# A fused chunk-selected attention and SwiGLU kernel: hand-woven instruction order replaced by a list-scheduled order with explicit buffers, with 64x64-tile chunk bounds and 256-token FFN blocks

## The chip, the cores and the metric

The kernel runs on one core of one Trainium2 chip. The metric is the device time of one execution in microseconds (us), and lower is better. Every execution has a state: fast, or slow when it is over 1.5% longer than the fastest execution of the same kernel; a single execution has none. A kernel is called faster or slower only where the whole 95% interval of its ratio lies more than 2% from 1. "Span" is the time from the first to the last instruction of the profiled execution; it is about 1.7 us shorter than the device time.

The engines are named as in the profile: PE is TensorE (matmuls) and PEld its weight loads, DVE is VectorE, ACT is ScalarE, POOL is GpSimd, SP is SyncE, which issues most of the loads and all of the stores. The program gives each engine its instructions in a fixed order; the second dip below shows GpSimd standing still for 4.96 us with a later instruction ready.

## The reference, cut to what matters

There are 4 batches, 8 heads, 768 tokens and 64 elements per head. Keys are in 24 chunks of 32. Each query attends to at most 6 chunks, those with the largest upper bound of the score. The result, as 3072 tokens of 512, goes through RMS normalisation and a SwiGLU layer of width 1536.

```python
k_min, k_max = min and max of k over each chunk of 32 tokens
ub = np.sum(np.maximum(q * k_min, q * k_max), axis=-1)      # one bound per query and chunk
ub = np.where(causal, ub, -1e9)
top_chunks = np.argsort(ub, axis=-1)[..., -6:]
scores = q @ k.T / 8, masked to the chosen chunks and to the past
attn = softmax(scores);  x = attn @ v
xn = x / sqrt(mean(x * x) + 1e-6) * rms_g
out = (silu(xn @ w_gate) * (xn @ w_val)) @ w_out
```

The unit of work is a *job*: 256 tokens of one batch and 4 of its heads (24 jobs). Two jobs make one 256-token *block* (12 blocks), and a block that has been through attention can go through the FFN.

## The kernel before

Loads come as 2 KB runs per partition (8 tokens of 64 elements), VectorE transposes them to head dimension by token, and GpSimd or ScalarE makes a bf16 copy.

```python
in_=src[b, 4 * g + a, BLK * m:BLK * (m + 1), :].rearrange(
    "(r j) d -> r (j d)", r=32, j=8)                       # 2 KB runs
...
def p_transpose(j, nm):
    nc.vector.transpose(
        out=st[j][nm + "T"].rearrange("p h (r j) -> p j h r", r=32, j=8),
        in_=st[j][nm + "raw"][:])
```

The chunk bounds are a product of queries with a block-diagonal matrix BD of the chunks' minima and ranges, in fp32, on the whole 128x128 array. Four heads use 32 rows each, so three quarters of BD are zeros.

```python
def p_upper(j):
    for t in range(4):
        rhs = st[j]["qT"][:, t, BLK - w:] if t < 2 else st[j]["qR"][:, t - 2, :]
        nc.tensor.matmul(ubp[:, 0:w], bd[:, t, :], rhs, start=(t == 0), stop=(t == 3))
```

The FFN works on 256 or 512 tokens at a time. Its matmuls are cut into *slices* (one gated pair of columns, or one projection), and the main loop puts one slice after each piece of attention work, by hand:

```python
CHUNKS = [(0, 1), (1, 1)] + [(2 + 2 * i, 2) for i in range(4)] + [(10, 1), (11, 1)]   # blocks
...
for i in range(2, NU):                 # units of attention, batch after batch
    need(nxt); scores(nxt)
    sl = next_slice(i)
    sl and sl.part()                   # FFN matmuls on PE
    if nxt: exps(nxt, 0)
    prep()                             # transposes, bounds and ranking of a later job
    sl and sl.part()
    if nxt: exps(nxt, 1)
    sl and sl.rest()
    run_later()                        # normalisation of a finished block, some steps later
    ...
    values(u, 0, avn, [kg], pts)
    if last: normalise(u, 0, avn)
    ...
```

The softmax here doesn't subtract the row's maximum and nothing guards it: scores larger than these inputs give would overflow.

## Time and profile before

The kernel took 366.86 us, the median of three executions (366.36 to 367.74; 366.89 with a fourth that was run beside the changed kernel).

| Engine | busy, us | share of span |
|---|---|---|
| PE | 308.3 | 84% |
| DVE | 216.1 | 59% |
| POOL | 201.1 | 55% |
| ACT | 198.7 | 54% |

These are the lines of its page that the argument rests on. The first is busy time, share and instruction count per engine. The next three cut the span into 40 slices of 9.1 us and give, in tenths, the busy share of PE, the clock granted to PE, and the share of the DMA engines.

```profile
PE 308.3 (84%) x3132; PEld 197.0 (54%) x3168; DVE 216.1 (59%) x539; ACT 198.7 (54%) x321; POOL 201.1 (55%) x327
PE   0255597889969799799879997999999999999995
PEclk9999978996998999999969999999999999999999
DMA  7999955536243233222430321210000200011001
```

PE is the bound, but it does little in the first five slices, where the DMA engines are full, and it has gaps until about slice 25. A busy PE is also not a PE at its rate. The timeline of PE shows the same eight matmuls early and late (start, length, group, and in brackets the idle time before and what ended it):

```profile
32.66 1.87 PE L397 MATMUL gp<-xsT,wg 128*128 128x256 bf16 x8 [1.31 <-DVE xsT L376]
...
93.05 1.05 PE L397 MATMUL gp<-xsT,wg 128*128 128x256 bf16 x8
```

The late group is followed by the next one 0.89 us after its start, so eight such matmuls cost 0.87 to 0.89 us when the array is warm, and about twice that at 32 us. The Trainium skill ("TensorE: Matmul & The Clock Gate", Part 1) says that the array starts at half its clock and gets the full one after some 3.4 us of sustained work. The trace agrees in the ratio; no run here isolates the 3.4 us.

I therefore use a second measure beside busy time, called *work*: each matmul counted at its warm, back-to-back duration from this trace (0.109 us for 256 columns on the full array, 0.216 for 512, and so on; for the new bounds, which it does not have, the figure in the change). The program has 272 us of such work. In a stretch of time, work over length is the *efficiency*, and length minus work is the *loss*, which contains idle time and half-rate time alike. Before, the loss is 365.2 - 272 = 93 us. (The 272 counts the eight narrow bounds jobs, of 64 columns, in proportion to their columns, at 0.43 us; the trace shows 0.84 us for a warm one, at 139.60 us. The work is thus nearer 275 us and the loss nearer 90. The prediction and the sums below keep 272 and 93; where the 3 us matter, it is said.)

The last line needed here is a group of VectorE (line, operation, shapes, count, then busy us and mean ns):

```profile
L179 DVE STREAM_TRANSPOSE kT<-kraw 128x512 f32<-128x512 f32 x24 | 26.3, 1096 | 0.4 <-DMA kraw<-in_k_dram 0.4
```

### The profile page before, as it was taken

How to read it: one execution, taken by the hardware profiler on the slowest of the kernel's cores; microseconds unless marked ns; L12 is line 12 of the kernel's file. 1: busy time of each engine (PE TensorE's matmuls, PEld its weight loads, DVE VectorE, ACT ScalarE, POOL GpSimd, SP SyncE). 2: the span in 40 equal slices, each digit the busy share in tenths (PEclk: the TensorE clock that was granted, in tenths of full speed). 3: DMA queues.
4: the chain of work that ended last, by engine and by line, in shares of the span. 5: the costliest groups of instructions: out<-in, count | busy, mean ns of one | idle time of the engine just before them, and what ended most of it. 6: DMA issues, size and time to landing. Idle time of an engine off the chain costs nothing.

```text
span 365.2 us, 8414 instructions
## 1 busy us (share of the span) xinstructions
PE 308.3 (84%) x3132; PEld 197.0 (54%) x3168; DVE 216.1 (59%) x539; ACT 198.7 (54%) x321; POOL 201.1 (55%) x327
## 2 busy tenths in 40 slices
PE   0255597889969799799879997999999999999995
PEld 0243375556856465455554554556546555548682
DVE  6336726677786787775576887538875144404130
ACT  2322444455744557684429576456783588735461
POOL 6362454636785556866347768339874064713361
PEclk9999978996998999999969999999999999999999
DMA  7999955536243233222430321210000200011001
GB/s 155 193 205 196 208 146 148 133 87 177 62 111 84 75 108 89 65 58 74 154 102 22 83 59 29 86 61 2 2 2 30 86 3 2 2 72 44 31 31 57
DMA packets 43305, 30.44 MB, mean 83 GB/s; under 512 B 29440, under 2 KB 34048, under 8 KB 43264
## 3 DMA queue, kind: packets, MB, share of 16 engines
q1 hardware_dynamic: 38160, 24.66, 24.6%
q0 software_dynamic: 4720, 4.72, 8.1%
q8 instruction: 25, 0.41, 0.5%
q10 hardware_dynamic: 384, 0.52, 0.4%
q14 instruction: 16, 0.13, 0.1%
HBM read 28.31 MB, written 6.29 MB: 95 GB/s over the span
## 4 chain that ended last, share of the span: by engine, by line
PE 63%; DVE 10%; DMA 10%; ACT 9%; issue 3%; POOL 2%; SPq 1%; DVEq 0%; ACTq 0%; POOLq 0%
PE op L420 16%; PE gp L397 14%; PE vp L397 13%; PE ubp L231 8%; DMA vraw<-in_v_dram 6%; PE sc L278 5%; PE avn L317 4%; DMA kraw<-in_k_dram 3%; ACT junk L346 3%; ACT th L404 3%; ACT pt L297 2%; DVE tg L410 2%; PE sc L283 2%; DVE qT L179 1%; PE tp L374 1%
## 5 line engine op out<-in xcount | busy, mean ns | idle before, releaser
L297 ACT ACTIVATE pt<-sc 128x768 bf16<-128x768 f32 (+1 forms) x96 | 85.7, 913 | 77.4 <-PE sc L283 77.2
L414 POOL TENSOR_TENSOR hh<-tg,vs 128x512 bf16<-128x512 bf16 x72 | 83.4, 1158 | 60.9 <-ACT vs L407 52.8
L410 DVE SCALAR_TENSOR_TENSOR tg<-th,gp 128x512 bf16<-128x512 bf16 x72 | 49.3, 685 | 69.2 <-ACT th L404 63.1
L397 PE MATMUL vp<-xsT,wv 128*128 128x512 bf16 (+1 forms) x384 | 77.2, 336 | 3.8 <-DVE tg L410 3.4
L397 PE MATMUL gp<-xsT,wg 128*128 128x256 bf16 (+1 forms) x361 | 76.4, 341 | 2.2 <-DVE xsT L376 1.3
L420 PE MATMUL op<-wo,hh 128*128 128x512 bf16 x275 | 64.2, 379 | 1.1 <-issue 0.3
L397 PEld LDWEIGHTS <-wv 128*128 128x128 bf16 x384 | 39.0, 102 | 30.9 <-issue 5.1
L407 ACT ACTIVATE vs<-vp 128x512 bf16<-128x512 f32 x72 | 43.2, 600 | 13.5 <-PE vp L397 12.1
L404 ACT ACTIVATE th<-gp 128x512 bf16<-128x512 f32 x72 | 43.1, 599 | 10.9 <-PE gp L397 10.4
L397 PEld LDWEIGHTS <-wg 128*128 128x128 bf16 x384 | 35.3, 103 | 22.6 <-issue 5.6
L301 POOL TENSOR_SCALAR_AFFINE_SELECT pt<-pt 128x512 bf16<-128x512 bf16 x48 | 31.1, 651 | 28.6 <-ACT pt L297 22.3
L420 PEld LDWEIGHTS <-hh 128*128 128x128 bf16 x288 | 26.7, 98 | 31.5 <-POOL hh L414 1.3
L317 PEld LDWEIGHTS <-pt 128*128 128x128 bf16 x672 | 31.2, 101 | 19.7 <-DVE xnat L332 5.2
L278 PE MATMUL sc<-qb,kb 32*128 32x256 bf16 (+1 forms) x768 | 35.8, 272 | 2.3 <-ACT pt L297 2.3
L427 ACT ACTIVATE osb<-op 128x512 f32<-128x512 f32 x24 | 14.3, 597 | 41.4 <-PE op L420 35.2
L283 PE MATMUL sc<-mt,chunkrow 32*128 32x256 bf16 (+2 forms) x384 | 25.1, 259 | 7.5 <-DVE mt L256 7.5
L179 DVE STREAM_TRANSPOSE kT<-kraw 128x512 f32<-128x512 f32 x24 | 26.3, 1096 | 0.4 <-DMA kraw<-in_k_dram 0.4
L179 DVE STREAM_TRANSPOSE qT<-qraw 128x512 f32<-128x512 f32 x24 | 26.4, 1098 | 0.0
L331 DVE RECIPROCAL rden<-avn 128x4 f32<-128x4 f32 x48 | 8.4, 175 | 29.5 <-PE avn L317 29.3
L278 PEld LDWEIGHTS <-kb 32*128 32x128 bf16 x768 | 16.3, 96 | 12.0 <-issue 9.2
L218 POOL TENSOR_SCALAR qraw<-qT 128x512 f32<-128x512 f32 (+1 forms) x24 | 12.3, 512 | 18.5 <-DVE qT L179 13.4
L231 PE MATMUL ubp<-qT,BD_180 128*128 128x256 f32 (+1 forms) x48 | 12.3, 385 | 10.9 <-POOL BD_180 L206 6.8
(129 smaller groups left out, 368.8 us busy)
## 6 DMA issues: line engine op xcount, KB each, us to landing
vraw<-in_v_dram SPq DMA_DIRECT2D x48, 128.0 KB, 2.7
out_dram<-osb SPq DMA_DIRECT2D x24, 256.0 KB, 2.1
kraw<-in_k_dram SPq DMA_DIRECT2D x92, 64.0 KB, 2.3
qraw<-in_q_dram SPq DMA_DIRECT2D x92, 64.0 KB, 1.9
wg<-in_moe_w_gate_dram POOLq DMA_DIRECT2D x3, 512.0 KB, 6.8
wv<-in_moe_w_val_dram POOLq DMA_DIRECT2D x3, 512.0 KB, 9.4
wo<-in_moe_w_out_dram POOLq DMA_DIRECT2D x1, 1536.0 KB, 22.3
kraw<-in_k_dram ACTq DMA_DIRECT2D x4, 64.0 KB, 2.3
```

Of the source, the lines that this page charges most:

```text
L179: nc.vector.transpose(out=st[j][nm + "T"].rearrange("p h (r j) -> p j h r", r=32, j=8), in_=st[j][nm + "raw"][:],)
L231: nc.tensor.matmul(ubp[:, 0:w], bd[:, t, :], rhs, start=(t == 0), stop=(t == 3))
L278: nc.tensor.matmul(o, st[jk]["kb"][r, t, ks], st[jq]["qb"][r, t, q0:], start=(t == 0), stop=False, skip_group_check=True,)
L283: nc.tensor.matmul(o[:, m0 - q0:], chunkrow[r, BLK * kg + P * e:BLK * kg + P * (e + 1)], st[jq]["mt"][r, m0:], start=False, stop=True, ski ...
L297: nc.scalar.activation(out=pt[:, hs, 0:W], in_=u["sc"][hp][:, :, 0:W], func=ACT.Exp, scale=SCALE)
L317: nc.tensor.matmul(avn[:, a, :], pts[kg][:, a, off:off + P], vext[:, e, a, :], start=(kb == 0 and a == 0), stop=(kb == nkb - 1 and a == 3) ...
L397: nc.tensor.matmul(ps[:, i * W:(i + 1) * W], w[:, g, ht * P:(ht + 1) * P], x[:, g, 0:W], start=(g == 0), stop=(g == NP - 1), skip_group_ch ...
L404: nc.scalar.activation(out=th[:], in_=gp[:], func=ACT.Tanh, scale=0.5)
L407: nc.scalar.activation(out=vs[:], in_=vp[:], func=ACT.Copy, scale=0.5)
L410: nc.vector.scalar_tensor_tensor(out=tg[:], in0=th[:], scalar=1.0, in1=gp[:], op0=ALU.add, op1=ALU.mult,)
L414: nc.gpsimd.tensor_tensor(out=hh[hp][:], in0=tg[:], in1=vs[:], op=ALU.mult)
L420: nc.tensor.matmul(op[:], hh[ht // K][:, o:o + P], wo[:, ht, :], start=(ht == 0), stop=(ht == NHT - 1),)
```

## The change

The intent is to fill PE's idle time. The change writes down every operation with an engine, an estimated duration, its inputs and its buffers, and lets a small scheduler inside the kernel play the program through before anything is emitted. At each step it takes, on the engine that can start first, the operation of best priority among those that can start at once. It also models the DMA rings, so that the order accounts for when loads land. The order that results is fixed; on the chip, engines and semaphores follow it. With that come four other changes: blocks are taken in a free order over the batches (small ones of all four batches first), FFN blocks are always 256 tokens (the first in two halves), the bounds use 64x64 tiles, and keys and queries from the fourth block on are loaded as 256 B runs in an element order that VectorE transposes faster.

```diff
+class Plan:
+    def run(self, in_order=()):
+        ...
+        while len(order) < len(self.ops):
+            best = None
+            for e, c in cand.items():
+                rows = [(est(o, e), o) for o in c]          # earliest start of each candidate
+                t0 = max(at[e], min(t for t, o in rows))
+                t, o = min(((t, o) for t, o in rows if t <= t0 + 1e-9),
+                           key=lambda r: (r[1].pri, r[1].seq))
+                if best is None or (t0, o.pri) < (best[0], best[1].pri):
+                    best = (t0, o, e)
+            ...
+            o.start = t; at[e] = t + o.occ; o.done = t + o.lat
+            if o.dma is not None:
+                rings.add(t + o.occ + 0.8, e, packets, cost, o)   # lands 1.0 us after its last packet
...
-    order = [(b, m, g) for b in range(B) for m in range(NBLK) for g in range(NG)]
+    ORDER = [(0, 0), (1, 0), (2, 0), (3, 0), (0, 1), (1, 1), (0, 2), (2, 1), (1, 2),
+             (3, 1), (2, 2), (3, 2)]
+    PACE, LEAD = 23.0, 60.0
+    SPLIT = {0}                  # the first block goes through the FFN in halves
+    PACKED = {0, 1, 2}           # blocks loaded as 2 KB runs; the others as 256 B runs
...
+        occ = {"SP": 0.46, "ACT": 0.46, "POOL": 0.9}[eng]          # modelled issue time of a DMA
...
-                    "(r j) d -> r (j d)", r=32, j=8),
+                        "(j r) d -> r j d", r=32)                  # 256 B runs, 16 packets of 0.022
...
-            nc.tensor.matmul(ubp[:, 0:w], bd[:, t, :], rhs, start=(t == 0), stop=(t == 3))
+            for t in range(4):
+                for hp in range(2):
+                    for c in range(2):
+                        TE.matmul(o[64 * c:64 * (c + 1), hp, 0:32 * nj],
+                                  d[64 * hp:64 * (hp + 1), t, :],
+                                  qs[t // 2][64 * hp:64 * (hp + 1), t % 2, :, c, :], ...)
...
+            plan.op(f"scale{i}{s}", "DVE", 0.265, 0.35, ...)        # each operation with occupancy
+            o = plan.op(f"{nm}{U}.{hp}", "PE", 0.873, 1.035, ...)   # and latency, in us
...
+    for o in plan.run(in_order=("kraw", "qraw", "vraw", "kT", "qT", "kb", "qb", "VX", ...)):
+        o.fn()
```

With 64x64 tiles the masks come out in two operands of half the width, one of which needs a copy between partitions (`swap`), so the mask matmuls are twice as many and half as wide. Eighteen of the 72 gate products move from GpSimd to VectorE.

## The prediction

> **What bounds the kernel now.** I costed every TensorE instruction of the old program at the warm, back-to-back duration that the instruction groups and timeline show: gate/value matmuls 0.109 us (256 columns) or 0.216 (512), projection 0.216, a four-at-a-time score or mask matmul 0.027, a value matmul 0.032, a 256-column fp32 bounds job 1.73. That is 272 us of a span of 365.2: TensorE is the bound, yet for 93 us it is idle, cold or throttled. By stretches of time, the work done is 10.6 us in 0-50, 35 in 50-100, 36 in 100-150, 71 in 150-240, 53 in 240-300, 19 in 300-320: efficiencies of 0.21, 0.70, 0.72, 0.79, 0.89, 0.95. In the first 45 us the DMA engines are full (share 0.9 to 1.2), the first FFN matmul comes at 32.7 us, and matmuls run at half rate (eight take 1.82 us until 49 us, 0.87 later). VectorE, ScalarE and GpSimd are busy 54 to 59%: none binds.
>
> **What changes.**
> 1. Bounds: 64x64 tiles, four at once, 128 columns instead of 256. This line is 8% of the chain of waits (31 us in total); I estimate half, so 12 to 15 us less, nearly all critical.
> 2. Masks cover only needed columns, from two half-width operands: no more PE time, twice the instructions.
> 3. FFN in 256-token blocks (the first in halves): same columns, 1248 weight loads instead of 768, hidden at 0.87 us per eight: +1 us. PE work becomes about 258 us. Tiling-mode changes on PE rise from 95 to 139 in instruction order; at about 0.1 us each, +4.5 us.
> 4. VectorE: key/query transposes in another element order, costed by the change at 0.6 us (1.1 now): 18 us less if right. 18 products move from GpSimd (1.16 us) to VectorE; swap copies and 16 more ScalarE row operations cost some 15 us. VectorE rises to about 75% of the shorter span; none binds.
> 5. Loads from block 4 on come as 256 B runs instead of 2 KB: more DMA time, harmless later, where the share is 0.2 to 0.4.
> 6. The order: small blocks of four batches first, FFN from about 18 us, every engine list-scheduled. This is the large term. Later loads wait behind weights, so I expect 15 us of PE work by 40 us: a loss of 25 us, against 39 in the first 50 today; afterwards efficiency 0.93, which the old kernel reaches only late.
>
> **Sum.** 40 + (258-15)/0.93 = 301, plus output copy and store (0.6 + 2.1 us) and some throttling: **307 us**, 80% range **296 to 322**. Faster by over 2%: 0.96; within 2%: 0.03; slower: 0.01.
>
> The Trainium skill ("TensorE: Matmul & The Clock Gate", Part 1) says matmuls start at half clock and reach full rate after about 3.4 us of sustained work; the trace agrees (1.82 against 0.87 us per eight).
>
> **What would show it.** Bounds matmuls near 16 to 19 us; eight 256-column matmuls still 0.87 us; efficiency above 0.9 from 50 us on, PE about 90% busy in the slices after the sixth; span minus PE work about 48 us instead of 93. If step 6 is wrong, middle slices show PE idle with waits on VectorE or ScalarE.
>
> **What would make it wrong.** The order is fixed from modelled durations: if VectorE or GpSimd run longer than modelled, or weights land later, in-order queues pass the delay on (over 320). If the clock stays up and gaps vanish, 295.

## The result, and the profile after

The changed kernel took 323.72 us, the median of four executions (322.84 to 324.64), against 366.89 us for the kernel before. The ratio is 0.8824, with a 95% interval of 0.8803 to 0.8846. Ratios here are the mean time of one kernel's fast runs over that of the other's of the same rounds, so they are not quite the ratio of the medians quoted. The direction and most of the size were as predicted; the time was 16.7 us above the predicted 307 and 1.7 us above the range.

These are the same lines of the page after; a slice is now 8.1 us.

```profile
PE 290.6 (90%) x4624; PEld 218.8 (68%) x4624; DVE 219.5 (68%) x613; ACT 219.3 (68%) x393; POOL 150.8 (47%) x270
PE   0459959989999997699999999999999999999894
PEclk9999969999999999799999999999999999999999
DMA  8999977666587567740120130100100100100101
```

PE is full from slice 18 (about 140 us) on. Two dips stand out before that: the sixth slice (40 to 48 us), where the granted clock is also low, and slices 16 and 17 (near 130 us). The transposes, which the by-shape view gives, and the wait list of PE (what waited, for what, total us, times, longest) are:

```profile
L487 DVE STREAM_TRANSPOSE kT<-kraw 128x512 f32<-128x512 f32 x24 | 18.6, 794 | 5.8 <-DMA kraw<-in_k_dram 5.4 <-POOL kb L495 0.2
```

```profile
PE S L618 <- ACT qb L494: 11.4, 1, 11.4
PE F L754 <- DVE xs L744: 5.1, 4, 2.5
PE F L824 <- POOL hh L814: 5.1, 1, 5.1
```

The first wait is the start of the program. The other two hold the two dips. Here is the first of them in PE's timeline:

```profile
43.03 0.61 PE L754 MATMUL F<-ident,xs 128*128 128x128 bf16 x4 [2.47 <-DVE xs L744]
44.19 0.61 PE L754 MATMUL F<-ident,xs 128*128 128x128 bf16 x4 [0.55 <-DVE xs L744]
45.36 2.32 PE L792 MATMUL F<-xsT,wg 128*128 128x256 bf16 x8 [0.56 <-ACT xsT L763]
47.47 2.97 PE L824 MATMUL F<-wo,hh 128*128 128x512 bf16 x8
...
55.79 1.04 PE L792 MATMUL F<-xsT,wv 128*128 128x256 bf16 x8
```

PE waits for the second block's normalisation, and then runs its next groups at half rate: eight gate matmuls take 2.1 us to the start of the next group, where the warm group of the same shape takes 0.87. The profile's chain of waits (`--critical`) leads from there back to a load of keys; three of its pieces (start, length):

```profile
32.20 7.20 DMA kraw<-in_k_dram
39.42 1.27 DVE kT L487 x2
41.91 0.41 DVE xs L744
```

The load landed at 39.40 us, and VectorE transposed its keys before it scaled the block that PE waited for. But GpSimd's step of the same normalisation ended only at 41.71 us, 0.2 us before the scalings, so the load is not shown to be the only cause.

The second dip needs three engines' timelines. PE:

```profile
125.69 1.06 PE L694 MATMUL F<-VX,pt 128*128 128x65 bf16 x28
131.84 4.30 PE L824 MATMUL F<-wo,hh 128*128 128x512 bf16 x12 [5.08 <-POOL hh L814]
```

GpSimd, for which PE waits:

```profile
123.92 0.61 POOL L495 CAST kb<-kT 128x512 bf16<-128x512 f32 x1
129.50 1.17 POOL L600 CAST VX<-vraw 128x512 bf16<-128x512 f32 x2 [4.96 <-DMA vraw<-in_v_dram]
130.63 1.15 POOL L814 TENSOR_TENSOR hh<-tg,vs 128x512 bf16<-128x512 bf16 x1
```

And SyncE, which issues the load that GpSimd waits for:

```profile
112.34 6.22 SPq L365 DMA_DIRECT2D kraw<-in_k_dram  x8
118.67 5.09 SPq L365 DMA_DIRECT2D qraw<-in_q_dram  x8
123.86 1.14 SPq L365 DMA_DIRECT2D vraw<-in_v_dram  x2
```

Read from the bottom: SyncE issued the value load of block (3, 1) at 123.86 us, after sixteen key and query loads that held it for 11.3 us: thirteen of them for 0.38 to 0.46 us each, three for 1.50 to 1.72 us. GpSimd had the two value casts in front of the gate product `hh` in its queue, so it sat 4.96 us with work that could have run (the product's last input, from ScalarE, was there at 124.8 us). PE needed that `hh` for its projection, stood for 5.08 us, and then ran twelve projections in 4.30 us, where twelve warm ones take 2.6.

The scheduler's own plan is a useful second trace, since its starts can be printed when the kernel is built. It has that value load issued at 109.5 us (14.4 us earlier) and the whole program done at 307.1 us. Comparing PE's starts of projections and of block transposes with the plan, the chip is 1.5 us late at 23 us, 7 to 9 us late from 51 to 124 us, 16 us late from 138 us, and 15.6 us late at the last projection: it lost nothing more to its plan in the last 180 us. SyncE was already 10.3 us late when the sixteen loads began (112.34 us against 102.05). Part of that came through the first dip: SyncE stood still for 2.7 and 1.0 us before the stores at 77.37 and 80.77 us, whose output PE had made about 7 us late. That is read from the timeline and was not tested.

The accounting of work by stretch (computed from PE's groups in each stretch as said above; matmuls across a boundary count in both):

| Stretch, us | work | efficiency | loss |
|---|---|---|---|
| 0 to 40 | 15.8 | 0.40 | 24.2 |
| 40 to 60 | 12.5 | 0.62 | 7.5 |
| 60 to 120 | 52.8 | 0.88 | 7.2 |
| 120 to 140 | 12.8 | 0.64 | 7.2 |
| 140 to 300 | 151.1 | 0.94 | 8.9 |
| 300 to end | 16.8 | 0.73 | 6.1 |

In total the work went from 272 to 260.5 us and the loss from 93 to 62 us. So of the 42 us of span, 11 are less work and 31 are less loss; with the narrow bounds jobs at their measured 0.84 us, 15 and 28.

### The profile page after: what moved, and what is told of

It is laid out like the page before. It is cut to its first block, busy times and chain, and to the rows that moved or that the text cites. A ratio compares the mean times of both kernels' runs of the same rounds, so it can differ in the third digit from the quotient of the medians.

```text
span 322.9 us, 11287 instructions
## 1 busy us (share of the span) xinstructions
PE 290.6 (90%) x4624; PEld 218.8 (68%) x4624; DVE 219.5 (68%) x613; ACT 219.3 (68%) x393; POOL 150.8 (47%) x270
## 3 DMA queue, kind: packets, MB, share of 16 engines
q1 hardware_dynamic: 69712, 24.66, 31.3%
## 4 chain that ended last, share of the span: by engine, by line
PE 64%; DMA 11%; DVE 9%; ACT 5%; SPq 4%; issue 3%; POOL 3%; DVEq 0%; POOLq 0%; ACTq 0%
PE F L792 29%; PE F L824 16%; DMA kraw<-in_k_dram 6%; PE S L549 5%; PE S L618 5%; PE F L694 5%; DMA vraw<-in_v_dram 4%; SPq L365 4%; PE S L629 2%; PE F L754 2%; DVE kx L502 1%; DVE xs L744 1%; POOL hh L814 1%; DVE kT L487 1%; ACT pt L668 1%
## 5 line engine op out<-in xcount | busy, mean ns | idle before, releaser
L668 ACT ACTIVATE pt<-S 128x1024 bf16<-128x1024 f32 (+3 forms) x100 | 86.5, 889 | 17.9 <-PE S L629 15.5
L792 PE MATMUL F<-xsT,wg 128*128 128x256 bf16 (+1 forms) x624 | 77.5, 269 | 1.5 <-ACT xsT L763 1.1
L792 PE MATMUL F<-xsT,wv 128*128 128x256 bf16 (+1 forms) x624 | 75.6, 267 | 0.5 <-DVE xnat L713 0.3
L824 PE MATMUL F<-wo,hh 128*128 128x512 bf16 x288 | 69.9, 390 | 5.1 <-POOL hh L814 5.1
L803 DVE SCALAR_TENSOR_TENSOR tg<-th,F 128x512 bf16<-128x512 bf16 x72 | 48.7, 677 | 34.9 <-ACT th L799 34.7
L799 ACT ACTIVATE th<-F 128x512 bf16<-128x512 f32 x72 | 43.6, 606 | 11.9 <-PE F L792 10.1
L618 PE MATMUL S<-qb,kb 32*128 32x256 bf16 (+1 forms) x784 | 34.5, 259 | 12.4 <-ACT qb L494 11.4
L811 ACT ACTIVATE vs<-F 128x512 bf16<-128x512 f32 x54 | 32.9, 609 | 6.2 <-PE F L792 4.3
L502 DVE TENSOR_REDUCE kx<-kT 128x16 f32<-128x512 f32 x48 | 30.3, 663 | 0.0
L694 PE MATMUL F<-VX,pt 128*128 128x65 bf16 x672 | 27.7, 195 | 2.2 <-ACT vs L811 0.9
L487 DVE STREAM_TRANSPOSE kT<-kraw 128x512 f32<-128x512 f32 x24 | 18.6, 794 | 5.8 <-DMA kraw<-in_k_dram 5.4
```

Source lines behind the costliest of these rows:

```text
L502: plan.op(f"ext{n}{J}", "DVE", 0.585, 0.67, lambda n=n, op=op: VE.tensor_reduce(out=at(kx)[:, n], in_=at(kT).rearrange("p h (c t) -> p h c ...
L618: TE.matmul(s[a // 2][:, a % 2, c0:c0 + q1 - q0], kbt[r, t, ks], qbt[r, t, q0:q1], start=(t == 0), stop=(t == 1 and not mask), skip_group_ ...
L668: lambda pt=pt, hs=hs, c0=c0, c1=c1, x=sc[hp]: SE.activation(out=at(pt)[:, hs, c0:c1], in_=at(x)[:, :, c0:c1], func=ACT.Exp, scale=SCALE), ...
L694: TE.matmul(o[:, a, :], p_[:, a, off:off + P], vt[:, e, a, :], start=(kb_ == 0 and a == 0), stop=(kb_ == nkb - 1 and a == 3), skip_group_c ...
L792: TE.matmul(at(p_)[:, n * W:(n + 1) * W], w[:, g, ht * P:(ht + 1) * P], at(xT)[:, g, 0:W], start=(g == 0), stop=(g == NP - 1), skip_group_ ...
L799: plan.op(f"tanh{U}.{hp}", "ACT", 0.48, 0.6, lambda th=th, gp=gp: SE.activation(out=at(th), in_=at(gp), func=ACT.Tanh, scale=0.5), pri, re ...
```

## The experiments

Three questions were open. Which part of the change brought the gain? Where did the 16.7 us go that I had not expected? And were the two dips accidents, or signs of something in the plan? My first theory was that the two dips cost their length and that the value load behind GpSimd's queue made the second. The rivals were that the 256 B runs slow everything, that the array's cold clock does, and that the plan's figures for loads make it too hopeful everywhere.

All runs gave the reference's results. Runs of different sets were each timed against the kernel before on their own chip, so ratios are compared between sets. Not tested apart were the FFN blocks of 256 tokens, the eighteen moved gate products, and the explicit buffers, which all variants of the new kernel share.

### The value casts behind the urgent product

```diff
+    order = plan.run(...)
+    late = [o for o in order if o.name in ("vx(3, 1, 0)", "vx(3, 1, 1)")]
+    order = [o for o in order if o not in late]
+    at_ = [o.name for o in order].index("hh(3, (0, 1)).5") + 1
+    order[at_:at_] = late
```

> One place of GpSimd's queue is changed: the two value casts of block (3,1), which waited for a load until 129.5 us, go behind the gated product hh that TensorE waited for (126.8 to 131.8 us). Theory A (an operation that is not urgent, but stands first in an in-order queue and waits for a late load, holds up the product): the 5.1 us wait shrinks to about 2 (the product's other input was ready at 127.3), the half-rate matmuls after it go, and the time falls from 323.7 by 4 to 6, to 318 to 320. Rival B (all engines wait for the late loads anyway): at most 1.5 less.

Measured: 322.1 us as the median of all four executions; the three fast ones took 321.56 to 322.37, with a median of 321.82. The ratio is 0.877 (0.8725 to 0.8816), against 0.8824. The profiled execution was the other one, and it was slow: 726.4 us. A profile of that tells nothing about the swap, so the kernel was run again for one look.

> The kernel of e1 again, for a trace of its fast state (the first one fell into an execution of 726 us). e1 gained 1.6 us, not 4 to 6. If another operation in an in-order queue, waiting for the same late loads, took over: TensorE's wait at 127 us is shorter than 5.1 us, and VectorE (next for it: a key transpose that waited for a load until 131.2 us) or GpSimd makes it wait again within 20 us, in sum about 5 us. If the wait was as long as before, the product had another reason.

Measured: 320.88 us in one execution (so its state is unknown, but it lies beside e1's fast ones), a span of 319.1. GpSimd's queue now runs the product first, and waits less long for the values:

```profile
123.89 1.15 POOL L814 TENSOR_TENSOR hh<-tg,vs 128x512 bf16<-128x512 bf16 x1 [0.45 <-ACT vs L811]
126.29 1.17 POOL L600 CAST VX<-vraw 128x512 bf16<-128x512 f32 x2 [1.25 <-DMA vraw<-in_v_dram]
```

PE's 5.1 us wait is gone, but a new one has come a little later in its timeline:

```profile
132.58 0.77 PE L754 MATMUL F<-ident,xs 128*128 128x128 bf16 x8 [2.01 <-DVE xs L744]
```

(My first expectation was wrong on when the product could run: the input that I had seen at 127.3 us belongs to the next block.) The loss between 120 and 140 us fell only from 7.2 to 5.1 us, or to 4.7 with the two projections that this trace's records lack there. So the mechanism of the second dip is shown, and its worth is about 2 us, not the 7 that PE's trace shows there: when one wait was taken away, the next thing that was late took its place. As a cause of the miss, then, the second dip by itself accounts for about an eighth of the 16.7 us.

As for the slow execution, its page has this as busy time, and its timeline has the following group of gate matmuls:

```profile
PE 702.4 (97%) x4624; PEld 395.3 (55%) x4624; DVE 218.2 (30%) x613; ACT 228.3 (32%) x393; POOL 150.5 (21%) x270
...
400.07 2.64 PE L792 MATMUL F<-xsT,wg 128*128 128x256 bf16 x8
```

All other engines have their usual busy time, while groups of eight gate matmuls took 2.1 to 2.5 us from start to start, 2.4 to 2.8 times the warm 0.87, from 60 us to the end. The clock recorded for it is 1.00. (The record is not always silent: of the kernel before, one execution in the same set was slow as well, 476.65 us, at a recorded clock of 0.671.) Nothing is concluded from these two executions for the change.

### The schedule's figures for loads

Only numbers of the scheduler's model change: the time that SyncE needs for an issue, the time of a packet in a ring for the 256 B runs, and the time from the last packet to the landing. The work of every engine stays the same, apart from operations that the plan may give to one of two engines.

```diff
-            op.done = now + 1.0
+            op.done = now + 1.5
-        occ = {"SP": 0.46, "ACT": 0.46, "POOL": 0.9}[eng]
+        occ = {"SP": 0.60, "ACT": 0.46, "POOL": 0.9}[eng]
-                        "r j h d -> r j (h d)"), 16, 0.022))
+                        "r j h d -> r j (h d)"), 16, 0.032))
```

> Only the schedule's model of loads is changed, to what the trace shows: 0.60 us of SyncE per load instead of 0.46, a ring packet of 256 B runs 0.032 instead of 0.022, landing 0.5 us later. No instruction is added or taken away; the order changes. Its own model ends at 303.6 us (307.1 with the old figures). Theory A (the stall at 127 us comes from a load model that is too fast): no wait over 2 us on TensorE between 100 and 300 us, and 310 to 316. Rival C (the mid stall is not a matter of the load model): 320 to 325.

Measured: 313.96 us (313.18 to 314.61), ratio 0.8552 (0.8513 to 0.8592), about 10 us less than the changed kernel. PE's slices have neither dip:

```profile
PE   0469979997999999999999999999999999998994
```

No wait on PE after 100 us is over 2 us. The start of the second block's FFN comes 3.1 us earlier and at full rate (VectorE now scales that block at 38.60 us, ahead of the two key transposes):

```profile
42.26 1.03 PE L792 MATMUL F<-xsT,wg 128*128 128x256 bf16 x8 [1.67 <-DVE xsT L767]
```

By the same accounting, the loss fell from 7.5 to 3.1 us in 40 to 60 and from 7.2 to 1.2 us in 120 to 140, and stayed within 1.1 us of the old value in the other stretches up to 300 us. That is where the two dips were. The two parts of the edit were then run apart.

> Of e2's three figures only the first: 0.60 us of SyncE per load instead of 0.46. The model ends at 307.1 us. If the issue time of SyncE is what the old model missed: 312 to 317. If it is the time in the rings and to landing: 320 to 325, with a wait of TensorE of 2 us or more between 60 and 160 us.

Issue time alone: 320.24 us (318.41 to 322.0), ratio 0.8699 (0.8648 to 0.8751).

> Of e2's three figures only the other two: a ring packet of 256 B runs 0.032 instead of 0.022 us, landing 1.5 us after the last packet instead of 1.0. The model ends at 303.7 us (e2: 303.6). If the rings are what matters: 311 to 316 as e2. If the issue time is: 320 to 325.

Packet and landing time alone: 312.69 us (312.16 to 315.27), ratio 0.8524 (0.8474 to 0.8575). So these two figures, which were not run apart, do nearly all of it, and the issue time alone brings 3.5 us (4.6 by the ratios). By the accounting of work, the issue time alone takes away the second dip (1.3 us of loss from 120 to 140) but not the first (6.9 us from 40 to 60), and from 140 to 300 it loses 3.5 us more than the changed kernel: taking away the second dip is again worth less than its length. The wait of 2 us or more between 60 and 160 us that I had expected with such a time did not come; the longest is 1.5 us. Packet and landing time alone leave 4.1 and 2.6 us of loss in the two stretches.

I had thought of these figures as the truer ones, and the profile bears that out only in part. How long a load of keys holds SyncE in the changed kernel, in ns (shortest, median, longest), is in this line:

```profile
L365 SPq DMA_DIRECT2D kraw<-in_k_dram x82: 311/448/3311, 1.3 to 136.0; - x82
```

So 0.46 was right for most loads: 140 of SyncE's 164 key and query loads took 0.50 us or less. The mean is 0.55 us, and my 0.6 was such a mean of groups of eight; 18 loads of 0.8 to 3.3 us raise it. What held those, the profile does not show. And the page's mean time of a packet on the hardware queue of the changed kernel is 31.3% of 16 engines' 322.9 us over 69,712 packets, which is 23 ns, close to the old 0.022; and the median time from issue to landing of a key load is 2.6 us, which is what the old model gives too (0.46 + 0.8 + 16 x 0.022 + 1.0). What the model lacks, by these figures, is the tail: the few long issues, and loads that wait for their turn. Making every load later in the plan is a stand-in for it. Whether a truer model of the queues would do better than a uniformly pessimistic one, no run tells.

### All keys and queries in 2 KB runs

```diff
-    PACKED = {0, 1, 2}
+    PACKED = set(range(12))
```

> All blocks load keys and queries as 2 KB runs with 4 transfers per tensor, as blocks 0 to 2 do, instead of 256 B runs with 8; the transposes of blocks 3 to 11 take 1.1 us instead of 0.7 on VectorE. If the 256 B runs and the number of transfers make SyncE late (it was 14 us behind its plan at 124 us): SyncE keeps its plan, no stall at 127, about 312 to 317. If VectorE is the tighter one up to 130 us (busy 80 to 100%): 321 or more, with waits on VectorE.

Measured: 322.94 us (322.29 to 323.39), ratio 0.8797 (0.8757 to 0.8836): the same as the changed kernel within the intervals. VectorE is busy for 238.3 us instead of 219.5, because the slower transposes come back, and the stall at 127 us does not appear. Thus the 256 B runs, as such, are not the cause of the miss: without them the same time is lost in other places (7.9 us of loss from 40 to 60, and 11.5 instead of 8.9 from 140 to 300). The result lies in the range that I had given for VectorE as the tighter engine, but PE's waits for VectorE's scalings (`xs`) are 6.3 us instead of 5.1, too little to show it. The faster transpose of the 256 B runs brings nothing in the end either.

### The bounds, twice

```diff
-            for t in range(4):
+            for t in list(range(4)) * 2:
-        o = plan.op(f"upper{J}", "PE", 0.925 if m else 0.49, 1.09 if m else 0.66, ...)
+        o = plan.op(f"upper{J}", "PE", 1.85 if m else 0.98, 2.02 if m else 1.15, ...)
```

> The 64x64 bounds matmuls are issued twice (same result, the accumulation is started again), and the schedule is told so: 18.7 us more TensorE work by the plan's figures, bounds then cost about what the 128x128 form did (31 us). If TensorE bounds the kernel after 40 us: 11 to 18 us more, 335 to 342. If its work hides in gaps: under 5 more.

Measured: 336.28 us (334.05 to 337.0), ratio 0.9146 (0.9083 to 0.9208), which is 12.6 us more (11.8 by the ratios). The bounds' busy time on PE rose from 23.9 to 43.9 us, which happens to be what they had in the kernel before (43.8). By the plan's figures that is 18.7 us more work (16 jobs of 0.925 and 8 of 0.49). So about two thirds of bounds work shows in the time, in the new order, where the scheduler had been told of it.

### The old kernel with the new bounds

The old kernel's order was kept, and the 64x64 bounds, the half-width masks and the copies between partitions (on VectorE) were put into it. Its diff is long; this is the core.

```diff
-            nc.tensor.matmul(ubp[:, 0:w], bd[:, t, :], rhs, start=(t == 0), stop=(t == 3))
+            for hp in range(2):
+                for c in range(2):
+                    nc.tensor.matmul(ubp[hp][64 * c:64 * (c + 1), 0:32 * nj],
+                                     bd[64 * hp:64 * (hp + 1), t, :],
+                                     qs[t // 2][64 * hp:64 * (hp + 1), t % 2, :, c, :],
+                                     start=(t == 0), stop=(t == 3))
...
+        nc.vector.tensor_copy(mto[0:64, 0:nj], mtd[64:128, 0, 0:nj])
+        nc.vector.tensor_copy(mto[64:128, 0:nj], mtd[0:64, 1, 0:nj])
```

> The old kernel with one part of the change: bounds on 64x64 tiles (two PSUM banks, swap copies on VectorE, masks from two half-width operands); order and all else as before. TensorE loses 12 to 15 us of bounds work, VectorE gains about 12 us. If the bounds matmuls were critical in the old order (8% of its chain of waits): 8 to 13 us less, 354 to 359. If its gaps would swallow it: within 4 us of 367.

Measured: 373.7 us (371.08 to 376.1), ratio 1.0204 (1.0138 to 1.0269): longer by 1.4 to 2.7%, so not clearly more than 2%. Both of my ranges had it shorter or within 4 us. The page shows the exchange:

```profile
PE 301.9 (82%) x4091; PEld 190.0 (51%) x4128; DVE 240.1 (65%) x627; ACT 198.7 (54%) x321; POOL 198.4 (54%) x327
```

PE is busy for 6.4 us less than before, VectorE for 24 us more. By PE's wait list, waits on VectorE's `xnat` grew from 5.4 to 8.1 us, and those on `tg` before the bounds grew from one of 1.2 us to nine of 4.9 us in all. One caution is that the bounds here take two of the three PSUM banks that they share with the FFN, where the changed kernel has them elsewhere; the extra banks may be part of the loss. What is shown is that this part of the change, put into the old order in this form, brings no gain, and costs some us.

### Batches in order

```diff
-    ORDER = [(0, 0), (1, 0), (2, 0), (3, 0), (0, 1), (1, 1), (0, 2), (2, 1), (1, 2), (3, 1), (2, 2), (3, 2)]
+    ORDER = [(b, m) for b in range(B) for m in range(NBLK)]
```

> The new kernel with its blocks in the order of the old one (batch after batch), list-scheduled by the same model, whose end is 306.6 us (307.1 in free order). If the free order over batches is a large term: 333 or more, as large attention blocks come while the weights are still landing. If the list schedule makes up for the order: within 6 us of 323.7.

Measured: 323.1 us (322.0 to 323.84), ratio 0.8801 (0.8756 to 0.8846). The free order over the batches, which the change names first, is worth nothing that these runs can see. The same order was also run with the later loads of the second experiment:

> The batch order of e7 with the load model of e2; its own model ends at 306.7 us (e7: 306.6). e2 may have won 10 us because its load model is nearer to the chip, or because any new order is a new draw. If the load model: this run comes 5 to 11 us below e7's 323.1, at 312 to 318, and TensorE has no stretch of 20 us between 60 and 300 us that loses over 3.5 us. If it was a draw: within 4 us of 323.

Measured: 315.31 us (314.9 to 315.83), ratio 0.8611 (0.8576 to 0.8646), 7.8 us less than the 323.1 of its pair (7.0 by the ratios, which count here, as the two ran on different chips). By its trace the stretch from 80 to 100 us loses 5.4 us, more than the 3.5 that I had allowed; but 21 projections, 4.5 us of work, are missing from its records, so that half of the expectation stays open. A new plan changes the order everywhere, so one gain of 10 us might have been a lucky draw. This second draw, from another order of blocks, speaks against that.

### Filling PE's early gaps with idle work

Wherever the plan leaves PE idle for over 0.5 us before 60 us, matmuls of the identity with itself are put in front of the next group that takes a fresh PSUM buffer; they are overwritten.

```diff
+        if o.eng == "PE":
+            gap, end = o.start - end, o.start + o.occ
+            if gap > 0.5 and o.start < 60.0 and o.takes:
+                ...
+                for _ in range(int((gap - 0.2) * 0.8 / 0.107)):
+                    TE.matmul(x, ident[:], ident[:], start=True, stop=True, skip_group_check=True)
```

> The new kernel with idle TensorE time before 60 us filled by matmuls whose result is overwritten (identity times identity, into the PSUM slot that the next operation fills), about 80% of each gap of the plan over 0.5 us. If part of the 31 us lost in the first 50 us is half clock after idling: eight 256-column matmuls at 45 us take 1.0 to 1.3 us instead of 2.3, the first 128-column groups 1.06 instead of 1.89, and 3 to 6 us less, 318 to 321. If the start is bound by loads and chains of small operations alone: within 1.5 us of 323.7.

Measured: 321.7 us (319.72 to 323.02), ratio 0.8761 (0.8703 to 0.8819). The first FFN matmuls now run at full rate (sixteen of 128 columns in 1.05 us, where they took 1.89), but the group at 45.39 us still takes 2.32 us, since the fillers there were too few. The time is 2 us less, but the intervals overlap, and it misses the 318 to 321 that I had expected. So filling these gaps is not shown to bring anything, and what the half rate after 42 us costs was not tested.

### A plan that knows no durations

```diff
+            o.occ, o.lat = 0.6, 0.8      # for every operation, in the model only
```

> The new kernel with a schedule that is blind to durations: every operation is taken to last 0.6 us (0.8 to its result); order of blocks, priorities, loads and work are unchanged. If modelled durations are what the list schedule lives on: TensorE waits all along, 335 or more. If priorities, many small operations and explicit buffers do it: 320 to 330.

Measured: 371.12 us, the median of the three fast executions (368.12 to 372.86; the fourth, 374.21, is slow), ratio 1.0122 (1.0047 to 1.0198). Everything else of the change is in it, yet it is no faster than the old kernel. Its slices and the head of its wait list on PE:

```profile
PE   0329969899689967998996998998999985699895
```

```profile
PE S L619 <- ACT pt L669: 18.0, 21, 1.8
```

PE is interrupted throughout, mainly by score matmuls that wait for ScalarE's exponentials, 21 times.

### A plan by priority alone

In the scheduler, an operation may be chosen although it cannot start yet, so the window `t0 + 1e-9` becomes unlimited. My first edit was faulty: the model then let a chosen operation start before its inputs were there, so it optimised against wrong times.

```diff
-                t, o = min(((t, o) for t, o in rows if t <= t0 + 1e-9),
+                t, o = min(((t, o) for t, o in rows if t <= t0 + 1.0e9),
```

> The new kernel with its choice by priority alone: an engine takes the operation with the lowest number among those whose inputs are scheduled, even if it must wait for it, where the list schedule takes only what can start first. Its own model ends at 310.0 us (307.1). If choosing by start time is a large term: 330 or more, with waits of TensorE in every stretch. If not: 318 to 328.

Measured: 406.2 us (404.08 to 408.06), ratio 1.109 (1.1028 to 1.1153). The order is valid and the result right, but it answers no question that I had put. The mended version charges the wait:

```diff
-                if best is None or (t0, o.pri) < (best[0], best[1].pri):
-                    best = (t0, o, e)
+                if best is None or (t, o.pri) < (best[0], best[1].pri):
+                    best = (t, o, e)
```

> e11 mended: its edit also let the model start the chosen operation before its inputs were there, so its end of 310.0 us meant nothing. Now the chosen operation starts when it can; the model ends at 366.5 us (307.1 by start time). If the start-time rule is what the new order lives on: 370 to 395. If the modelled figure is far off and priorities alone nearly do: under 345.

Measured: 363.55 us (363.43 to 363.81), ratio 0.9896 (0.9853 to 0.9938), and the model itself had said 366.5. That lies between my two ranges (370 to 395, and under 345), nearer the first. With the same durations, priorities and all other parts of the change, but without the rule "take what can start now", 40 of the 43 us are gone. Its slices look much like those of the kernel before:

```profile
PE   0539467989979979979899987998997999899995
```

### A version with all that helped

The later loads of the second experiment, the fillers, and the last block's FFN in halves, so that its first half ends earlier:

```diff
-        return ((0,), (1,)) if i in SPLIT else ((0, 1),)
+        return ((0,), (1,)) if i in SPLIT or i == 11 else ((0, 1),)
```

> A try to beat both: e2's load model, the last block's FFN in two 128-token halves as the first (so that its first half can start before its second half is normalised), and the fillers of e8 in the first 60 us. Its model ends at 303.2 us (e2: 303.6). e8 gained 2 us, the tail after 300 us lost 6 and could give 1 to 3: 309 to 314 expected, against 314.0 for e2. If nothing of it is critical: 313 to 316.

Measured: 311.24 us (310.72 to 312.78), ratio 0.8507 (0.846 to 0.8555). It beats both kernels. Against the later loads alone (0.8552, 0.8513 to 0.8592) the intervals overlap, so what the other two parts add is not separated from nothing.

### What the plan promised and what the chip did

Since each variant carries a plan, its promised end can be set beside the measured median:

| Version | plan's end, us | chip, us | chip later by |
|---|---|---|---|
| the change | 307.1 | 323.7 | 16.6 |
| 2 KB runs throughout | 304.6 | 322.9 | 18.3 |
| batches in order | 306.6 | 323.1 | 16.5 |
| bounds twice | 318.6 | 336.3 | 17.7 |
| issue time only | 307.1 | 320.2 | 13.1 |
| packet and landing only | 303.7 | 312.7 | 9.0 |
| all load figures | 303.6 | 314.0 | 10.4 |
| the same, batches in order | 306.7 | 315.3 | 8.6 |
| priority alone (mended) | 366.5 | 363.6 | -2.9 |

Of the plans that take what can start now, those with the old packet and landing figures run 13 to 18 us late, whatever else is in them, and those with later landings 9 to 10 us late. The plan by priority alone is slower on paper than on the chip. On paper the plans with later loads are at most 3.5 us shorter than their pairs; most of their gain is that the chip keeps to them better.

## Why the prediction was right or wrong

**What bounds the kernel: right.** PE was the bound with 93 us of loss, and the gain came mostly from that loss, 31 of 42 us (28 with the narrow bounds jobs as measured). That the scheduler is the large term was right as well: without its rule the kernel runs at 363.6 us, and without durations at 371.1.

**Step 1, bounds: right in size, wrong as a gain by itself.** I expected 12 to 15 us less, nearly all critical, and 16 to 19 us for the matmuls. A 256-token job took 1.73 us of PE before; now it is 1.03 us from the start of the job to the start of the next group (111.73 to 112.76 us in PE's timeline), the change of mode included. Counted by jobs the bounds went from 31.2 to 18.7 us (the second at the plan's 0.925 and 0.49 us per job), within what I had expected. The 31.2 contains eight narrow jobs at 0.43 us; at their measured 0.84 us it is 34.4, and the saving 15.7 us. The profile's windows, for the bounds' lines alone, give busy times that include pipelining (stretch, its length, PE and PEld busy with counts); before:

```profile
0.00:365.20 365.20, 43.80 (x192) 35.10 (x192) 0.96 0.34 83
```

and after:

```profile
0.00:322.90 322.90, 23.90 (x768) 19.59 (x768) 0.98 0.42 95
```

Putting the work back cost 12.6 us in the new order, so about two thirds of it is critical there. In the old order the same change of the bounds came with 24 us more VectorE work, and brought no gain.

**Steps 2 and 3, masks and FFN blocks: right.** A gate group still takes 0.87 us from start to start (43.13 after 42.26 in the trace with later loads), with 4624 weight loads instead of 3168. PE's work came to 260.5 us, 2.5 above the expected 258. Mode changes on PE were not tested apart, and the work does not contain them. The trace before prices one: a full bounds job takes 1.73 us up to the next group when that is in the same mode, and 1.83 us when it is in another. At 0.1 us each, the 138 changes of the new kernel (94 before) are by this estimate some 14 of its 62 us of loss. The prediction named the 4.5 us that they add, but its sum leaves them out.

**Step 4, VectorE: nearly right.** It was busy for 68% of the span, not 75, and the transposes took 0.79 us, not 1.1 (a mean; those in the new element order alone take about 0.70, where the change had 0.6). My 18 us for them was 15 (26.3 + 26.4 before, 18.6 + 18.8 after). That VectorE does not bind holds for its total, but not at 42 us, where PE waited for its scalings.

**Step 5, loads: "harmless later" failed in part.** The runs in themselves are harmless, as the run with 2 KB runs throughout shows. But SyncE's queue, in which single loads took up to 3.3 us instead of the modelled 0.46 and stores waited for late output, was 14.4 us behind its plan at one value load, and an in-order queue on GpSimd passed that on to PE. I had put such a delay, for weights and for slow engines, under "what would make it wrong" and had not costed it.

**Step 6: this is the step that failed.** "15 us of PE work by 40 us: a loss of 25 us" was right: 15.8 and 24.2. "Afterwards efficiency 0.93" was not: this term of the sum was mis-sized. After 40 us the sum of the prediction allowed 307 - 40 - 243 = 24 us of loss; the trace has 282.9 us with 244.7 us of work, hence 38.2 us of loss, an efficiency of 0.865. Together with 1.7 us more work (244.7 against 243) that is the 15.9 us between 307 and the span of 322.9. From 140 to 300 us the efficiency is 0.944, better than I said. The error sits in two stretches of 20 us, with efficiencies of 0.62 and 0.64: at 0.93 they would have lost 2.8 us together instead of 14.7. I had taken the best efficiency that the old kernel reaches, at its end, when all loads are done, and applied it to a stretch in which SyncE issues loads almost without a pause (loads and stores fill 95 of the 101 us from 38 to 139, by its own timeline). The waits were on VectorE in the first stretch, as the prediction's own sign for a wrong step 6 says, and on GpSimd in the second, which it does not name. With loads planned later, 10 of the 14.7 us come back, and the time with them (312.7 to 314.0) is 6 to 7 us above the prediction and inside its range.

**What stays open.** Why VectorE's two scalings at 42 us took 2.22 us, when 24 of them average 0.52 us each, is not settled. Nor is it settled which part of the gain of the later loads is truth in the figures and which is slack that happens to protect the plan. Each plan is also a new draw; the two plans with all load figures changed, which differ in the order of blocks, are 1.4 us apart, so differences of 1 to 2 us between plans should not be explained.

## What to carry to other kernels

A fixed order made by a list scheduler is worth as much as its rule and its durations: here neither the rule "take what can start now" nor the durations could be left out without losing nearly the whole gain, and the free order of blocks brought none. After that, the figures of the loads deserve care, because an in-order queue can turn one late load into idle time on engines that never touch its data; planning loads later cost little on paper here, and kept the chip nearer to the plan. When predicting such a change, compare plan and chip over the stretch in which loads still run, and expect that mending one visible stall gives back only part of its length, since the next late thing stands behind it.

## What the Trainium skill lacked or had wrong

- "DMA: Bandwidth & Descriptors" ("Issuing engines are not separate DMA queues") says that the time to initiate a DMA is usually small relative to the DMA itself. For one load the trace agrees: 0.45 us (median) of SyncE against 2.6 us from issue to landing for a 64 KB load of keys. It was not small in sum: loads and stores filled 95 of 101 us of SyncE, single loads held it for up to 3.3 us, and one value load came 14.4 us behind its plan. The page says nothing of what a busy issuer does to the loads behind it.
- The same page ("Specifications", and "Why small descriptors are slow (HBM only)") says that transfers under 512 B do not reach line rate. The trace agrees: for the same 24.66 MB the hardware queue took 24.6% of 16 engines' 365.2 us before and 31.3% of 322.9 us after, 90 against 101 us (92 in the run with 2 KB runs throughout). But the time was the same with and without the short runs (323.7 and 322.9 us), which the page does not lead one to expect or not to expect: it has no word on when this cost shows.
- "TensorE: Matmul & The Clock Gate" (Part 1) has, for one busy core, two states of the clock, full and half, and a caveat that the clock's events are unreliable and have been seen stuck at a quarter for 50 us or more. One execution here took 726.4 us, with eight gate matmuls in 2.1 to 2.5 us all through instead of 0.87, while its recorded clock was 1.00. That agrees with the caveat on records. The mean rate of about 0.37 lasts for a whole execution, and is neither of the page's two states; single matmuls followed each other after 0.24 or 0.38 us instead of 0.109, so it may be a mixture of states.
- "TensorEngine Tiling (Array Packing)" ("Overview", "Key Properties") gives up to a factor of 2 for a dimension of at most 64 and says that a change of mode drains the array. The bounds job went from 1.73 to 1.03 us per 256 tokens, the change of mode included, a factor of 1.7, which lies within that. The page ties each tile to its partitions, but does not say that results may therefore need copies between partitions: putting the tiles into the old order added 24 us to VectorE and made the kernel 1.4 to 2.7% longer.
